# Memory attention and a bilinear FFN on one core: turning the means of k and v by DMA instead of on TensorE

## The chip, the cores and the metric

The kernel runs on one core of one Trainium2 chip. The metric is the device time of one execution in microseconds (us); it was run three times. A core has five engines that work side by side, each on its own list of instructions, in order: TensorE (PE, matmuls; its weight loads are shown apart as PEld), VectorE (DVE), ScalarE (ACT), GpSimd (POOL) and SyncE (SP, which here only issues DMAs). PE writes to PSUM, which has eight banks; DVE and ACT read results from there. DMAs are issued by SyncE, ScalarE or GpSimd and carried by 16 DMA engines.

## The reference, cut to what matters

There are 8 batches, 8 heads, 576 tokens, head size 64 and 32 memory slots. `phi` decides how the tokens are averaged into 32 slots; attention then runs over those slots, and its output goes through two up projections, whose product goes through the down projection.

```python
a = np.exp(phi - np.max(phi, axis=2, keepdims=True))
a = a / (np.sum(a, axis=2, keepdims=True) + 1e-09)
k_m = np.einsum('bhsm,bhsd->bhmd', a, k)        # means of k: 32 x 64 for each head
v_m = np.einsum('bhsm,bhsd->bhmd', a, v)        # means of v
scores = scale * np.matmul(q, k_m.transpose(0, 1, 3, 2))
attn = softmax(scores)                          # over the 32 slots
x = np.matmul(attn, v_m)                        # then (B, S, H*D)
out = ((x @ w_a) * (x @ w_b)) @ w_out           # d_model 512, d_ff 1536
```

## The kernel before: the parts that matter here

The kernel never forms `x`. It multiplies the means of v into the up weights ("fold"), so that the up projection of a batch is the attention matrix `A` times a folded weight `vab`. Both the scores (which need the means of k) and the fold (which needs the means of v) take them with the head dimension on the partitions, so the means have to be turned. For batches 2 to 7 this is a chain of three units:

```python
def kv_sums():                      # "kv": 72 small matmuls, exp(phi) x (k, v, ones), into two PSUM banks
    t["pkv"] = [banks.take([P, 3, D], F32, "pkv", hold=True) for _ in range(2)]
    for i in range(NI):
        for g in range(2):
            for j in range(4):
                r, hp = head(g, j)
                nc.tensor.matmul(t["pkv"][g][0][32 * j:32 * j + 32], ..., tile_position=(64 * r, 32 * j))

def take_kv():                      # "km": divide by the sums, PSUM -> SBUF, on VectorE; frees the two banks
    t["rep"] = mid.tile([P, 2, 3, P], F16, name="rep")
    for g in range(2):
        pkv, bank = t["pkv"][g]
        nc.vector.reciprocal(out=t["rphi"][:, g:g + 1], in_=pkv[:, 2, 0:1])
        ...                         # two tensor_scalar: 128 x 256 and 128 x 128
        banks.free(bank)

def kv_transpose():                 # "kvt": six 128 x 128 transposes on TensorE, one VectorE copy out of PSUM
    t["kvT"] = mid.tile([P, 6, P], F16, name="kvT")
    pT = banks.tile([P, 6, P], F16, name="pT")
    for g in range(2):
        for x in range(3):
            nc.tensor.transpose(out=pT[:, ...], in_=t["rep"][:, g, x], identity=ident)
    nc.vector.tensor_copy(out=t["kvT"], in_=pT)
```

The matmuls of `kv`, of the fold (`v0` to `v2`) and of the scores (`sc`) use small tiles of the PE array (64 x 32 or 32 x 32 instead of 128 x 128). The fold and the scores read `kvT`:

```python
def fold(lo, hi, zs):               # "v0", "v1", "v2": 16 matmuls into four held banks
    if len(zs) > 1 and b > 2:
        work.settle()               # first bring the down product that holds a second bank to its end
    ...
def take_fold(lo, hi, z):           # "x0a" ... "x2b": one copy on ScalarE, one on VectorE; frees two banks
    for g, engine_copy in enumerate((nc.scalar.copy, nc.vector.tensor_copy)):
        ...
def scores(gs):                     # "sc": 32 matmuls into four held banks; "e0", "e1" take two each on ScalarE
```

The main loop is the up projection, half a batch at a time in 12 steps. One step is two matmuls `pa`, two matmuls `pb`, a copy of `pa` on ScalarE (`a_sb`) and a product on VectorE (`ht`). After each step come some matmuls of the down projection (`py`, `pv`, `px`; `work.advance`), and then the side units that the plan has in that slot. The side units prepare the next batch; a name with `'` is of the batch after that one. `qt` turns q on VectorE, `exp` is the exponential of phi, `den` and `nr` make the softmax's denominators, and `L` issues the loads of a later batch.

```python
for step in steps:
    for _ in up(*step):
        work.advance()
        next(side, us[step[0]]["-"])()

second = "v2_+x2a_+exp0 x2b_ exp1 - kv+km qt0 kvt+qt1 - qt2+qt3 sc+e0 e1+v0+x0a+x0b den0 ... x2b - qt2'+nr1+kv'+km' - - kvt'+qt3'"
every = "- sc+e0 e1 den0 v0+x0a+x0b - - nr0+exp0' - - v1+x1a qt0' x1b+den1 exp1' - v2+x2a+x2b nr1+qt1' kv'+km' qt2' - qt3' - kvt'+L -"
last = "sc+e0 - e1 - v0+x0b - x0a den1 - - den0 v1+x1b x1a+nr0 - - - - nr1+v2+x2a - - - - - x2b"
```

`second` runs during batch 2, `every` during batches 3, 4 and 5, `last` during batch 6. So the means of batches 3 and 4 are made in `second`, those of batches 5, 6 and 7 in `every` (`kv'`, `km'`, `kvt'`). PSUM banks are handed out in program order, the one freed longest ago first.

Of the kernel before, what the change touches and what calls it, by code (L numbers as in the profile page):

```python
# [8 lines left out]
F32 = mybir.dt.float32  # L9
F16 = mybir.dt.float16  # L10
# [3 lines left out]
P = 128  # L14
# [4 lines left out]
def kernel(  # L19
# [11 lines left out]
    nc = tc.nc  # L31
# [14 lines left out]
    mid = ctx.enter_context(tc.tile_pool(name="mid", bufs=2))  # L46
    small = ctx.enter_context(tc.tile_pool(name="small", bufs=2))
# [105 lines left out]
    ident = consts.tile([P, P], F16, name="ident")  # L153
# [32 lines left out]
    def units(b):  # L186

        u = {}
        t = {}
# [28 lines left out]
                            tile_position=(64 * r, 32 * j),  # L218
                        )

        def take_kv():

            t["rep"] = mid.tile([P, 2, 3, P], F16, name="rep")
            t["rphi"] = small.tile([P, 2], F32, name="rphi")
            for g in range(2):
                pkv, bank = t["pkv"][g]
                nc.vector.reciprocal(out=t["rphi"][:, g:g + 1], in_=pkv[:, 2, 0:1])
                km = pkv[:, 0].rearrange("p (d e) -> p e d", e=2).unsqueeze(2).to_broadcast([P, 2, 4, 32])
                vm = pkv[:, 1].unsqueeze(1).to_broadcast([P, 2, D])
                for out, x in ((t["rep"][:, g, 0:2].rearrange("p e (z d) -> p e z d", z=4), km),  # L230
                               (t["rep"][:, g, 2].rearrange("p (z d) -> p z d", z=2), vm)):
                    nc.vector.tensor_scalar(out=out, in0=x, scalar1=t["rphi"][:, g:g + 1], scalar2=None, op0=ALU.mult)
                banks.free(bank)

        def kv_transpose():

            t["kvT"] = mid.tile([P, 6, P], F16, name="kvT")
            pT = banks.tile([P, 6, P], F16, name="pT")
            for g in range(2):
                for x in range(3):  # L240
                    nc.tensor.transpose(out=pT[:, (2 * g + x, 4 + g)[x == 2], :], in_=t["rep"][:, g, x], identity=ident)
            nc.vector.tensor_copy(out=t["kvT"], in_=pT)

        def sums(g, x):

            if g == 0 and x == 0:
                t["kvm"] = mid.tile([P, 2, 2, D], F16, name="kvm")
                t["rphi"] = small.tile([P, 2], F32, name="rphi")
                t["kvT"] = mid.tile([P, 6, P], F16, name="kvT")
            part = (slice(0, 3, 2), slice(1, 2))[x]  # L250
            pk = banks.tile([P, 2 - x, D], F32, name="pk")
# [3 lines that stand above are left out]
                    nc.tensor.matmul(  # L255
                        pk[32 * j:32 * j + 32],
                        t["exp"][64 * r:64 * r + 64, hp, i, :],
                        kvs[b][64 * r:64 * r + 64, part, hp, D * i:D * (i + 1)],
                        start=(i == 0),
                        stop=(i == NI - 1),  # L260
                        tile_position=(64 * r, 32 * j),
                    )
            if x == 0:
                nc.vector.reciprocal(out=t["rphi"][:, g:g + 1], in_=pk[:, 1, 0:1])
            nc.vector.tensor_scalar(out=t["kvm"][:, g, x], in0=pk[:, 0], scalar1=t["rphi"][:, g:g + 1], scalar2=None,
                                    op0=ALU.mult)
# [86 lines left out]
        def one(f, *a):  # L353
            return lambda: f(*a)

        for z in range(2):
            u[f"exp{z}"] = one(exp_phi, z)
            u[f"ks{z}"] = one(sums, z, 0)
            u[f"kt{z}"] = one(transpose, z, 0)
            u[f"vs{z}"] = one(sums, z, 1)  # L360
            u[f"vt{z}"] = one(transpose, z, 1)
            u[f"s{z}"] = one(scores, (z,))
            u[f"e{z}"] = one(exp_scores, z)
            u[f"den{z}"] = one(denominators, z)
            u[f"nr{z}"] = one(normalise, z)
            for hf in range(2):
                u[f"den{z}{hf}"] = one(denominators, z, (hf,))
                u[f"nr{z}{hf}"] = one(normalise, z, slice(hf, hf + 1))
            for n in range(NCH):
                u[f"v{n}{'ab'[z]}"] = one(fold, 512 * n, 512 * (n + 1), (z,))  # L370
                u[f"x{n}{'ab'[z]}"] = one(take_fold, 512 * n, 512 * (n + 1), z)
            for n in range(2):
                u[f"hv{n}{'ab'[z]}"] = one(fold, 256 * n, 256 * (n + 1), (z,))
                u[f"hx{n}{'ab'[z]}"] = one(take_fold, 256 * n, 256 * (n + 1), z)
# [4 lines left out]
        u["sc"] = one(scores, (0, 1))  # L379
        u["kv"] = one(kv_sums)  # L380
        u["km"] = one(take_kv)
        u["kvt"] = one(kv_transpose)
        u["-"] = lambda: None
        return u

# [230 lines left out]
    def ups(steps, side=()):  # L616

        side = iter(side)
# [4 lines that stand above are left out]
        for f in side:  # L623
            work.advance()
            f()
# [5 lines left out]
    def half_steps(b, hf, lo=0):  # L631

        return [(b, i, (hf,)) for i in range(lo, NFF)]

    us = {b: units(b) for b in range(B)}

    def named(b, names):
# [6 lines left out]
    def slots(b, names):  # L644

        def both(fs):
            return lambda: [f() for f in fs]
        def unit(n):
            if n == "fin":
                return lambda: work.pull(-work.done % NFF)  # L650
            if n == "L":
                return lambda: load(b + 2) if b + 2 < B else None
            if n[0] == "y":
                return lambda: some(int(n[1:]))
            if n[0] == "d" and n[1:].isdigit():
                return lambda: work.pull(int(n[1:]))
            return us[b + n.endswith("'") - n.endswith("_")][n.rstrip("'_")]

        return [both([unit(n) for n in x.split("+")]) for x in names.split()]
# [30 lines left out]
    ups(half_steps(1, 0, 4), slots(1, "- v2a+x2a+v2b+x2b+qt0' - - qt1'+exp0' exp1'+qt2' - kv'+km'+y9"))  # L690
    work.plan(S + HALF, 10)
    ups(half_steps(1, 1, 4), slots(2, "qt3 kvt - sc+e0+e1 - den0+den1+nr0 - v0+nr1+x0a x0b - v1+x1b x1a"))
    second = "v2_+x2a_+exp0 x2b_ exp1 - kv+km qt0 kvt+qt1 - qt2+qt3 sc+e0 e1+v0+x0a+x0b den0 nr0+v1+x1a - x1b+exp0' L exp1' v2+x2a den1+qt0'+qt1' x2b - qt2'+nr1+kv'+km' - - kvt'+qt3'"
    every = "- sc+e0 e1 den0 v0+x0a+x0b - - nr0+exp0' - - v1+x1a qt0' x1b+den1 exp1' - v2+x2a+x2b nr1+qt1' kv'+km' qt2' - qt3' - kvt'+L -"
    last = "sc+e0 - e1 - v0+x0b - x0a den1 - - den0 v1+x1b x1a+nr0 - - - - nr1+v2+x2a - - - - - x2b"
    for b in range(2, B):
        if b == 2:
            load(4)
# [35 lines left out]
```

The softmax here doesn't subtract the row's maximum and nothing guards it: scores larger than these inputs give would overflow.

## Time and profile before

| | before |
|---|---|
| time, median of three (lowest to highest) | 243.41 us (243.34 to 243.49) |
| span of the profiled execution | 241.9 us |
| DMA: moved, mean rate | 34.12 MB, 141 GB/s |
| HBM read / written | 42.47 MB / 9.44 MB |
| copy of the turned means out of PSUM, 128 x 768 (DVE) | 6 times, median 554 ns |
| products of the means, `rep` (DVE) | 24 times, median 413 ns |
| loads of phi, k, v, q of one batch (issued by GpSimd) | 576 KB each; median issue to landing 6.8, 9.5, 10.2, 13.5 us |
| store of an output row block (issued by SyncE) | 128 KB, median 3.1 us |

An engine's busy time says how much of the span it worked. The chain of work is the one that ended last, followed back from the last instruction; each piece of it names an engine, the tile written and the source line, and `x72` is the number of instructions in the piece. A piece whose length is more than its instructions need holds a wait or a switch. In this trace the line numbers are those of the kernel before: L212 is the sums of k and v, L241 the transposes on TensorE, L292 the scores, L338 the fold, L466 the down products, L594 the up matmuls.

### The profile page before, as it was taken

What the parts mean: (1) busy time and instruction counts of PE and PEld (TensorE: products, weight loads), DVE (VectorE), ACT (ScalarE), POOL (GpSimd) and SP (SyncE); (2) the same over time, 40 slices, a digit from 0 to 9 for tenths busy, and PEclk for the clock granted to TensorE, in tenths of its full rate; (3) what the DMA queues carried; (4) which work ended last, traced back from release to release, by engine and by line L of the source; (5) the groups of instructions that cost most, each with busy time, mean ns of one, the idle gap of its engine ahead of it and who ended that gap; (6) DMA issues with size and microseconds to landing.
All of it is one profiled execution on the core that took longest, in us unless ns stands there. A gap on an engine that the chain in (4) does not pass through costs nothing.

```text
span 241.9 us, 7803 instructions
## 1 busy us (share of the span) xinstructions
PE 230.9 (95%) x3110; PEld 169.8 (70%) x3110; DVE 167.2 (69%) x406; ACT 157.2 (65%) x410; POOL 159.4 (66%) x135
## 2 busy tenths in 40 slices
PE   7769999999999999999999999999999999999993
PEld 7535664456757867777788777877787878888882
DVE  4635784569858869976984659875987586756642
ACT  2265761669697599598857777587856877565330
POOL 7953244599879539973989759882949087936001
PEclk9999999999999999999999999999999999999999
DMA  6999999999947943992269542795220303032154
GB/s 235 234 197 207 206 256 207 256 208 283 219 130 178 217 91 93 235 194 49 46 174 212 140 89 56 170 207 137 49 46 12 78 13 78 8 84 63 42 129 116
DMA packets 25764, 34.12 MB, mean 141 GB/s; under 512 B 2016, under 2 KB 19808, under 8 KB 25728
## 3 DMA queue, kind: packets, MB, share of 16 engines
q0 software_dynamic: 19264, 23.14, 51.6%
q1 hardware_dynamic: 5952, 9.70, 15.8%
q10 hardware_dynamic: 512, 0.79, 1.0%
q8 instruction: 24, 0.39, 0.7%
q14 instruction: 12, 0.10, 0.1%
HBM read 42.47 MB, written 9.44 MB: 215 GB/s over the span
## 4 chain that ended last, share of the span: by engine, by line
PE 88%; ACT 4%; DMA 3%; DVE 2%; issue 2%; DVEq 0%; POOLq 0%
PE pa L594 20%; PE pb L594 19%; PE py L466 17%; PE pv L466 8%; PE pva L338 5%; PE po L391 5%; PE px L466 4%; DMA phi_sb<-in_phi_dram 3%; PE pkv L212 2%; PE pscore L292 2%; PE pD L315 1%; PE pk L255 1%; ACT E L305 1%; ACT L L316 1%; PE pw L151 1%
## 5 line engine op out<-in xcount | busy, mean ns | idle before, releaser
L605 DVE TENSOR_TENSOR ht<-a_sb,pb 128x288 f16<-128x288 f16 x168 | 73.3, 448 | 36.2 <-ACT a_sb L602 26.9
L594 PEld LDWEIGHTS <-vab 128*128 128x128 f16 x768 | 71.5, 98 | 27.3 <-issue 9.4
L602 ACT CAST a_sb<-pa 128x288 f16<-128x288 f32 x168 | 66.9, 409 | 26.2 <-PE pa L594 24.7
L594 PE MATMUL pa<-A,vab 128*128 128x288 f16 x384 | 75.9, 287 | 0.2
L594 PE MATMUL pb<-A,vab 128*128 128x288 f16 x384 | 74.9, 286 | 1.0 <-ACT vab L350 0.5
L448 POOL TENSOR_TENSOR h_sums<-ht 128x768 f16<-128x768 f16 x28 | 45.9, 1642 | 32.9 <-DVE ht L605 32.5
L466 PEld LDWEIGHTS <-h_sums 128*128 128x128 f16 x384 | 37.3, 98 | 7.0 <-issue 0.5
L350 DVE CAST vab<-pva 128x512 f16<-128x512 f32 (+1 forms) x52 | 32.6, 644 | 4.6 <-PE pva L338 4.2
L350 ACT CAST vab<-pva 128x512 f16<-128x512 f32 (+1 forms) x52 | 28.1, 571 | 9.4 <-PE pva L338 9.2
L466 PEld LDWEIGHTS <-ht 128*128 128x128 f16 x288 | 28.1, 98 | 5.7 <-issue 0.4
L466 PE MATMUL py<-w_sums,h_sums 128*128 128x256 f16 x192 | 30.4, 272 | 0.0
L448 POOL TENSOR_TENSOR h_sums<-ht,h_sums 128x768 f16<-128x768 f16 x14 | 23.0, 1643 | 0.9
L448 POOL TENSOR_TENSOR h_sums<-h_sums,ht 128x768 f16<-128x768 f16 x14 | 23.0, 1642 | 0.9
L326 POOL TENSOR_TENSOR A<-E,R 128x576 f16<-128x576 f16 x12 | 15.3, 1279 | 7.5 <-ACT R L324 7.4
L305 ACT ACTIVATE E<-pscore 128x288 f16<-128x288 f32 x32 | 11.4, 417 | 12.3 <-PE pscore L292 12.2
L466 PE MATMUL pv<-w_sums,h_sums 128*128 128x256 f16 x96 | 16.2, 273 | 0.0
L466 PE MATMUL py<-wo_sb,ht 128*128 128x256 f16 x96 | 16.0, 273 | 0.0
L473 ACT ACTIVATE u<-py 128x256 f32<-128x256 f32 x32 | 12.6, 393 | 5.0 <-PE py L466 4.8
L466 PE MATMUL py<-w_sums,ht 128*128 128x256 f16 x96 | 15.5, 272 | 0.1
L466 PE MATMUL px<-wo_sb,ht 128*128 128x256 f16 x96 | 15.4, 273 | 0.0
L316 ACT ACTIVATE L<-pD 128x288 f32<-128x288 f32 x32 | 11.6, 429 | 5.1 <-PE pD L315 4.8
L194 ACT ACTIVATE exp_sb<-phi_sb 128x576 f16<-128x576 f32 x16 | 11.0, 705 | 5.6 <-DMA phi_sb<-in_phi_dram 5.6
(65 smaller groups left out, 280.5 us busy)
## 6 DMA issues: line engine op xcount, KB each, us to landing
out_dram<-o_sb SPq DMA_DIRECT2D x68, 128.0 KB, 3.1
phi_sb<-in_phi_dram POOLq DMA_DIRECT2D x8, 576.0 KB, 6.8
kv_sb<-in_v_dram POOLq DMA_DIRECT2D x7, 576.0 KB, 10.2
kv_sb<-in_k_dram POOLq DMA_DIRECT2D x7, 576.0 KB, 9.5
q_sb<-in_q_dram POOLq DMA_DIRECT2D x6, 576.0 KB, 13.5
wo_sb<-in_moe_w_out_dram POOLq DMA_DIRECT2D x6, 256.0 KB, 13.6
q_sb<-in_q_dram POOLq DMA_DIRECT2D x4, 288.0 KB, 10.0
wa_sb<-in_moe_w_a_dram POOLq DMA_DIRECT2D x2, 512.0 KB, 13.8
```

Of the source, the lines that this page charges most:

```text
L305: nc.scalar.activation(out=Ev[:, g, :, z, :], in_=pss, func=AF.Exp, scale=1.0 / (8.0 * CS))
L316: nc.scalar.activation(out=t["L", g][:, sl], in_=pD, func=AF.Ln)
L326: engine.tensor_tensor(out=attn[b][:, g, sl], in0=t["E"][:, g, sl], in1=t["R", g][:, sl], op=ALU.mult)
L338: nc.tensor.matmul(t["pva", lo, z][g][0][32 * j:32 * j + 32, 0:hi - lo], t["kvT"][64 * r:64 * r + 64, 4 + g, M * j:M * j + M], w_sbs[z][64 ...
L350: engine_copy(out=vabs[b][z][:, g, lo:hi], in_=pva[:, 0:hi - lo])
L391: nc.tensor.matmul(po, ht[:, i, P * c:P * (c + 1)], wo_sb[:, i, :], start=(i == 0), stop=(i == NFF - 1))
L448: engine.tensor_tensor(out=out, in0=in0, in1=in1, op=op)
L466: nc.tensor.matmul(po, lhs[:, i], rhs[:, i], start=first and i == 0, stop=i == KH - 1, skip_group_check=not first)
L473: nc.scalar.mul(out=x, in_=po, mul=scale)
L594: nc.tensor.matmul(ps, vabs[b][x][:, g, P * i:P * (i + 1)], attn[b][:, g, HALF * hf:HALF * (hf + 1)], start=(g == 0), stop=(g == 1))
L602: nc.scalar.copy(out=a_sbs[b, i, hf], in_=ps)
L605: nc.vector.tensor_tensor(out=ht[:, i, t0:t0 + HALF], in0=a_sbs.pop((b, i, hf)), in1=ps, op=ALU.mult)
```

## The change

The turn of the means of batches 5, 6 and 7 leaves TensorE. A new unit `kvd` issues one DMA transpose on SyncE's queue, from `rep` in SBUF to `kvT` in SBUF; `rep` gets the six blocks in the order of `kvT`, so that one transfer of 128 x 768 does all. The unit `km` can now be done one bank at a time (`km0`, `km1`). In `every`, the sums `kv'` come directly behind the fold `v1`, seven slots earlier than before, so that the transfer has time and so that two groups of 64 x 32 matmuls stand in one run. The other side units are placed anew in all three plans: `d1` to `d5` pull that many matmuls of the down projection into a slot. Batches 2 to 4 keep the transposes on TensorE.

```diff
-        def take_kv():
-            t["rep"] = mid.tile([P, 2, 3, P], F16, name="rep")
-            for g in range(2):
+        def take_kv(gs=range(2)):
+            if gs[0] == 0:
+                t["rep"] = mid.tile([P, 6, P], F16, name="rep")
+                t["rphi"] = small.tile([P, 2], F32, name="rphi")
+            for g in gs:
 ... (same operations; rep is now indexed 2 * g, 2 * g + 1 and 4 + g)
-            for g in range(2):
-                for x in range(3):
-                    nc.tensor.transpose(out=pT[:, (2 * g + x, 4 + g)[x == 2], :], in_=t["rep"][:, g, x], identity=ident)
+            for x in range(6):
+                nc.tensor.transpose(out=pT[:, x, :], in_=t["rep"][:, x], identity=ident)
             nc.vector.tensor_copy(out=t["kvT"], in_=pT)
+
+        def kv_turn():
+            t["kvT"] = mid.tile([P, 6, P], F16, name="kvT")
+            nc.sync.dma_start_transpose(out=t["kvT"], in_=t["rep"].rearrange("p x d -> p (x d)"))
+            u[f"km{z}"] = one(take_kv, (z,))
+        u["kvd"] = one(kv_turn)
-    second = "v2_+x2a_+exp0 x2b_ exp1 - kv+km qt0 kvt+qt1 - qt2+qt3 sc+e0 e1+v0+x0a+x0b den0 nr0+v1+x1a - x1b+exp0' L exp1' v2+x2a den1+qt0'+qt1' x2b - qt2'+nr1+kv'+km' - - kvt'+qt3'"
-    every = "- sc+e0 e1 den0 v0+x0a+x0b - - nr0+exp0' - - v1+x1a qt0' x1b+den1 exp1' - v2+x2a+x2b nr1+qt1' kv'+km' qt2' - qt3' - kvt'+L -"
-    last = "sc+e0 - e1 - v0+x0b - x0a den1 - - den0 v1+x1b x1a+nr0 - - - - nr1+v2+x2a - - - - - x2b"
+    second = "v2_+d1+x2a_+exp0 x2b_ exp1 - kv+km+d2 qt0 d4+kvt+qt1 - qt2+qt3+sc+e0 - e1+v0+d2+x0a+x0b den0+d3 exp0' v1+nr0+x1a x1b+qt0' L+d5 den1 v2+x2a exp1'+qt1'+x2b - - qt2'+kv'+nr1+km' - - qt3'+kvt'+d5"
+    every = "- sc+e0 e1 den0 nr0+v0+x0a+x0b - - exp0' exp1' - v1+x1b+x1a+kv'+km0'+d3 - den1+km1' kvd'+qt0' - - nr1+qt1' v2+x2a+x2b - qt2' - qt3' - - L"
+    last = "sc+e0 d3 - e1 v0+x0b - - den1 - - den0+d1 x0a+v1+x1b x1a+nr0 - - - v2+x2a - nr1 - - - - x2b"
```

More of the change, by code (lines that the diff above doesn't have):

```diff
@@ L219, in kv_sums @@
                         )
-        def take_kv():
-            t["rep"] = mid.tile([P, 2, 3, P], F16, name="rep")
-            t["rphi"] = small.tile([P, 2], F32, name="rphi")
-            for g in range(2):
+        def take_kv(gs=range(2)):
[3 more added lines that the diff above has]
+            for g in gs:
                 pkv, bank = t["pkv"][g]
@@ L229, in take_kv @@
                 vm = pkv[:, 1].unsqueeze(1).to_broadcast([P, 2, D])
-                for out, x in ((t["rep"][:, g, 0:2].rearrange("p e (z d) -> p e z d", z=4), km),
-                               (t["rep"][:, g, 2].rearrange("p (z d) -> p z d", z=2), vm)):
+                for out, x in ((t["rep"][:, 2 * g:2 * g + 2].rearrange("p e (z d) -> p e z d", z=4), km),
+                               (t["rep"][:, 4 + g].rearrange("p (z d) -> p z d", z=2), vm)):
                     nc.vector.tensor_scalar(out=out, in0=x, scalar1=t["rphi"][:, g:g + 1], scalar2=None, op0=ALU.mult)
```

## The prediction, made before the changed kernel was run

> **What bounds the kernel now.** I read the page's busy times first, then the chain that ended last by engine, then a table of stages, and then the chain itself, piece by piece, in two stretches.
>
> ```profile
> PE 230.9 (95%) x3110; PEld 169.8 (70%) x3110; DVE 167.2 (69%) x406; ACT 157.2 (65%) x410; POOL 159.4 (66%) x135
> ...
> PE 88%; ACT 4%; DMA 3%; DVE 2%; issue 2%; DVEq 0%; POOLq 0%
> ```
>
> TensorE is busy 95% of the span and carries 88% of the chain; the other engines stand at 65 to 70%. The stages (batch 2; its end; batches 3, 4, 5; 6 and 7; the tail) say where that holds:
>
> ```profile
> 72.50:87.00 14.50, 14.42 (x237) 10.60 (x235) 12.24 (x31) 10.28 (x28) 9.66 (x9) 1.00 0.99 201
> ...
> 101.00:127.00 26.00, 26.00 (x351) 19.95 (x350) 20.73 (x51) 19.41 (x51) 19.48 (x15) 1.00 0.59 123
> 127.00:155.00 28.00, 28.00 (x371) 21.86 (x369) 19.49 (x48) 19.73 (x52) 23.78 (x18) 1.00 0.61 122
> 155.00:181.00 26.00, 26.00 (x351) 19.82 (x349) 20.30 (x49) 19.61 (x53) 15.73 (x11) 1.00 0.59 125
> ```
>
> From 101 to 181 us PE is busy for every microsecond at full clock. No wait is left there to take away: what gets shorter there must be work of PE, or time that PE loses between two kinds of work. The chain shows both (start, length, engine, tile, line):
>
> ```profile
> 117.00 0.56 PE pva L338 x16
> 117.56 0.35 PE pa L594 x2
> 117.91 0.24 PE pb L594 x2
> 118.16 0.33 PE py L466 x3
> ...
> 119.30 0.87 PE pkv L212 x72
> 120.17 0.35 PE pa L594 x2
> 120.52 0.24 PE pb L594 x2
> ...
> 124.36 0.34 PE pT L241 x6
> 124.70 0.25 PE pa L594 x2
> ```
>
> A pair `pa` takes 0.24 us, but 0.35 right behind the small tiles of the fold or of the sums: leaving the small tiles costs 0.11. Behind the transposes it takes 0.25: 128 x 128 transposes cost no switch. In the same pattern for batches 6 and 7 the transposes stand at 154.22 and 179.48, again 0.34 long.
>
> The second stretch is batch 2, the only place after 75 us where the chain leaves PE before the tail:
>
> ```profile
> 84.63 0.40 PE pscore L292 x31
> ...
> 85.05 0.12 ACT E L305
> ...
> 85.76 0.30 ACT a_sb L602
> ...
> 86.09 0.47 DVE ht L605
> ...
> 86.59 0.41 PE pa L594 x2
> ```
>
> After the scores PE had one step (0.35 + 0.24) and a fold (0.56) to do, which ends at 85.03 + 1.15 = 86.18; it goes on at 86.59. So some 0.4 us are lost to the row exponentials, the copy and the product that must free PSUM banks.
>
> **What the Trainium skill says.** TensorEngine Tiling (Array Packing), section Tiling Modes: changing the tiling mode drains TensorE. The trace agrees: 0.11 us on leaving; the fold and the sums are both 64 x 32, so one behind the other should not drain. TensorE: Matmul & The Clock Gate, Part 4: PE-mode transpose: the output lands in PSUM and has to be copied, and one 128 x 128 transpose took about 275 ns in a kernel. Here six back to back take 0.34 us together, 57 ns each, and the measurement decides; the copy is there (554 ns on DVE). DMA: Bandwidth & Descriptors, section Latency and other measured facts: DMA transposes reached 261 GB/s with strided blocks, 350 to 400 when contiguous. No run here shows one yet. The same page, section Queues, rings and completion order: an engine serves the queues in turn, packet by packet, so that a transfer shares with the loads.
>
> **The change part by part.**
>
> *Transposes off PE.* Three groups of six transposes, 0.34 us each, all on the bounding engine: 3 x 0.34 = 1.02 us less. Three DVE copies of 0.55 go too (1.7 us of DVE), off the path and worth nothing by themselves.
>
> *Sums behind the fold.* In the new order of PE's instructions the 72 matmuls stand directly behind the 16 of `v1`, three times. Entering and leaving is paid once for both. Leaving is 0.11. Entering I take from the run itself: a group of eight 64 x 32 matmuls works side by side, a `pa` of 288 columns takes 0.12 us, so 0.42 ns a column; 72 x 192 / 8 columns are 0.72 us, and the run takes 0.87: 0.15 over. For the fold, 16 x 512 / 8 columns are 0.43 and the run takes 0.56: 0.13 over. So one pair of switches is 0.24 to 0.26 us, and 3 x 0.25 = 0.75 us go.
>
> *Batch 2.* Scores now stand one slot before the fold with an empty slot between, two products follow the fold and three the denominators. This should take most of the 0.4 us wait: 0.3 us less. The rest of `second` has no wait to remove.
>
> *What is moved and costs nothing if it fits.* The `d` units do not add matmuls, they take them from later slots. 3110 matmuls become 3092, the 18 transposes. The last 108 matmuls, behind the last up step, are in the same order as before, with their wait of about 1.3 us on DVE at 226 us; the tail stays. So does the start: up to 72 us nothing that runs is changed.
>
> *The DMA transpose.* 128 x 768 x 2 bytes are 197 KB. At the skill's 261 GB/s that is 0.75 us, to which I add the 3.1 us from issue to landing of a 128 KB store: an estimate of 3 to 5 us. The room it has: in batch 3 the fold `v1` stands at 112.34, so the sums run from 112.9 to 113.7. In the kernel before the products of `km` end 2.7 us after the sums begin (119.30 to 122.0); now the second half comes two slots later, about 4 us after: 117. The scores come at 128.46 less what was saved, say 127.5: 10 us of room. Batch 6: sums at 142.8, products done at 147, scores at 157.12 less 1.5: 8.5 us. Batch 7: 168, 172, and scores at 181.78 less 2: nearly 8 us. An estimate of 3 to 5 us fits in all three. The stores behind it on SyncE's queue come later by as much; four output buffers, two used per pair of blocks, leave them that time.
>
> *Inputs.* The sums come seven slots earlier, so k and v must have landed earlier. The load for batch 7 is issued from 152.1 to 155.2, and GpSimd's place for it hardly moves. The DMA share by stretches of 3 us is 1.19 at 162 to 165 and 0.40 at 165 to 168, so the last of the four (q) lands near 166 and v before; the sums want it at 168. For batch 5 the share is 0.02 from 111 on, wanted at 112.9; for batch 6 it falls to 0.47 from 135 on, wanted at 142.8. It fits, by 2 to 6 us.
>
> Sum: 1.02 + 0.75 + 0.3 = 2.1 us less, 241.3.
>
> **The rivals.**
>
> *The transfer is slow or delayed.* If turning 197 KB takes 12 us rather than 4, the scores wait about 2, 3.5 and 4 us, some 10 us together, because PE is in order and has no slack: 251. Against it speaks the care with which `kv'` was moved forward: nobody gives eight slots to a transfer of 2 us, but that also says that it is not short. For it speaks that no row of this profile shows a DMA transpose; and for batch 5 a transfer beyond 5 us would meet the load issued at 122.3 on all engines.
>
> *A pile-up behind `v1`.* Slot 10 now holds two copies on DVE (1.28), two on ACT (1.12), and the first half of the products (0.9 on DVE), the second half follows two slots later. A step needs 0.45 us of DVE in about 0.85. Counted from the end of the fold, DVE is done with the copies at 1.28, with the first half at 2.2, with two `ht` at 3.1, with the second half at 4.0. PE meanwhile does the sums (0.83), three products, two steps, two more products and the denominators, until 2.7. Its banks come free just ahead of it: the third step's `pb` needs the bank of the first `ht`, free at 2.65, and gets to it at 2.95. That fits by 0.3 us. If it does not, 0.3 us are lost three times, with like delays at slot 4, where `nr0` joins the copies on ACT: 242.5 in all.
>
> *Banks in `last`.* `x0a` now comes seven slots after its fold, so two more banks are held, and only four are left for the steps. The same count leaves 0.15 to 0.3 us a step. A loss here would be below 1 us.
>
> *The bound does not move but other waits grow with it.* DVE loses 1.7 us of work and ACT none, both below 75%, so no other engine becomes the bound.
>
> **Range and chances.** 241.3 if all fits; I add 0.3 for small waits that a new plan nearly always brings: 241.6 us, 0.7% less. The low end is all of the sum and all of the batch-2 wait, 240.8. The high end has the pile-up and one late transfer, 244.0. Faster by over 2% means under 238.5, more than there is to remove: 0.02. Slower by over 2% (above 248.3) needs the slow transfer: 0.05. Within 2%: 0.93.
>
> **What would show it.** In the chain after: no `pT` pieces after 105 us; `pkv` directly behind `pva`, the two together near 1.3 us, with one 0.35-like exit behind; PE at 100% in the stages of batches 3 to 5, each about 0.6 us shorter. The row of the DMA transpose should land in 3 to 5 us. I am wrong if `pscore` waits for `kvT`, if `pkv` waits for a load or for `exp`, or if `pa` or `pb` in the two steps behind `v1` wait for `rep`, `vab` or `ht`.

## The result and the profile after

The changed kernel takes 241.28 us (median of four, 241.15 to 241.93) against 243.38 us before: a ratio of 0.9919, 95% interval 0.9900 to 0.9937. The prediction was 241.6 us, in a range of 240.8 to 244.0.

Three lines of the profile of the changed kernel: busy times, the hardware DMA queue (packets, MB, share of 16 engines) and, from the table of DMA issues, the new transfer (count, median us from issue to landing).

```profile
PE 230.6 (96%) x3092; PEld 170.3 (71%) x3092; DVE 165.4 (69%) x403; ACT 158.7 (66%) x410; POOL 159.5 (67%) x135
...
q1 hardware_dynamic: 8352, 10.29, 18.4%
...
kvT<-rep SPq DMA_TRANSPOSE x3, 3.3
```

The 18 matmuls that are gone are the transposes. The queue carries 2,400 packets more than before (5,952), 800 for each transfer of 197 KB: they are small.

Two executions can stand up to a microsecond apart at a place that has the same work behind it (the sums of batch 3 begin at 77.66 us before, at 77.41 after, and between 77.2 and 78.2 in the runs below). For effects of 0.3 us the whole time is too coarse. So I compare two stretches, each between the starts of two pieces of the chain. Stretch A runs from the sums of batch 3 to the scores of batch 4, stretch B from there to the scores of batch 7. First the kernel before (both), then the one after (both): start and end, length and PE busy, the other engines' busy times, then PE's clock, DMA share and GB/s.

```profile
77.66:102.25 24.59, 24.51 (x415) 18.46 (x418) 21.13 (x55) 18.20 (x47) 17.93 (x14) 1.00 0.79 160
102.25:181.78 79.53, 79.53 (x1078) 61.26 (x1083) 59.63 (x144) 58.40 (x153) 58.47 (x43) 1.00 0.59 121
```

```profile
77.41:102.04 24.63, 24.55 (x418) 18.61 (x423) 21.19 (x55) 18.25 (x47) 18.28 (x15) 1.00 0.82 163
102.04:179.68 77.64, 77.64 (x1056) 60.49 (x1062) 57.71 (x140) 59.30 (x153) 58.16 (x42) 1.00 0.66 130
```

B is 1.89 us shorter, and PE is busy all the time in both. The two kernels do not have the same work in a stretch: by the order of PE's instructions, A has 74 down products before and 77 after, B 291 and 288 (the `d` units). Three products are 0.33 us in the chain. For the same work A is 0.29 us shorter and B 1.56 us: 1.85 us together. From the scores of batch 7 to the wait in the tail, both take 44.37 us. The rest of the difference of the medians, 2.10 us, is of the size by which the starts differ.

The chain of the changed kernel, at the place where fold and sums now meet:

```profile
111.79 0.56 PE pva L343 x16
112.35 0.76 PE pkv L212 x70
113.11 0.43 PE py L473 x3
```

The sums take 0.76 us here instead of 0.87, and only one exit is paid, by the products behind them (0.43 instead of 0.33). The list of SyncE in the same stage, and then the landings of the three transfers (least, median, most):

```profile
116.23 2.08 SPq L247 DMA_TRANSPOSE kvT<-rep  x1
```

```profile
DMA to landing us min/median/max: 2.7/3.3/3.7
```

The scores of batch 5 come at 127.37 us, so the transfer of batch 5 had 11.1 us and used 3.3; the 3.7 are of batch 6.

### The profile page after: what moved, and what is told of

The parts are those of the page before. It is cut to its first block, busy times and chain, and to the rows that moved or that the text cites. A ratio compares the mean times of both kernels' runs of the same rounds, so it can differ in the third digit from the quotient of the medians.

```text
span 239.6 us, 7764 instructions
## 1 busy us (share of the span) xinstructions
PE 230.6 (96%) x3092; PEld 170.3 (71%) x3092; DVE 165.4 (69%) x403; ACT 158.7 (66%) x410; POOL 159.5 (67%) x135
## 3 DMA queue, kind: packets, MB, share of 16 engines
q0 software_dynamic: 19264, 23.14, 52.2%
## 4 chain that ended last, share of the span: by engine, by line
PE 77%; DMA 16%; DVE 2%; issue 1%; POOL 1%; ACT 1%; DVEq 0%; POOLq 0%
PE py L473 18%; PE pa L601 18%; PE pb L601 17%; PE pv L473 9%; DMA wb_sb<-in_moe_w_b_dram 6%; DMA q_sb<-in_q_dram 5%; PE pva L343 5%; DMA kv_sb<-in_v_dram 4%; PE px L473 4%; PE po L398 2%; PE pkv L212 2%; PE pscore L297 1%; PE pD L320 1%; DVE ht L612 1%; ACT a_sb L609 1%
## 5 line engine op out<-in xcount | busy, mean ns | idle before, releaser
L601 PEld LDWEIGHTS <-vab 128*128 128x128 f16 x768 | 72.4, 98 | 24.9 <-issue 7.8
L473 PE MATMUL py<-w_sums,h_sums 128*128 128x256 f16 x192 | 31.3, 273 | 0.0
L473 PE MATMUL py<-wo_sb,ht 128*128 128x256 f16 x96 | 16.7, 273 | 0.0
L473 PE MATMUL px<-wo_sb,ht 128*128 128x256 f16 x96 | 15.9, 273 | 0.0
L321 ACT ACTIVATE L<-pD 128x288 f32<-128x288 f32 x32 | 11.5, 418 | 6.0 <-PE pD L320 5.8
L203 DVE STREAM_TRANSPOSE qT<-q_sb 128x288 f32<-128x288 f32 x32 | 14.6, 464 | 0.3 <-DMA q_sb<-in_q_dram 0.3
## 6 DMA issues: line engine op xcount, KB each, us to landing
kv_sb<-in_v_dram POOLq DMA_DIRECT2D x7, 576.0 KB, 10.3
```

The lines of the kernel that those rows point to most:

```text
L203: nc.vector.transpose(out=t["qT"][:, hp, :].bitcast(F32), in_=qs[b][:, hp, :].bitcast(F32))
L321: nc.scalar.activation(out=t["L", g][:, sl], in_=pD, func=AF.Ln)
L473: nc.tensor.matmul(po, lhs[:, i], rhs[:, i], start=first and i == 0, stop=i == KH - 1, skip_group_check=not first)
L601: nc.tensor.matmul(ps, vabs[b][x][:, g, P * i:P * (i + 1)], attn[b][:, g, HALF * hf:HALF * (hf + 1)], start=(g == 0), stop=(g == 1))
```

## The experiments

All runs are variants of the changed kernel; only the plans of the side units are edited. "Stretch A" and "B" are those above, and a comparison is always for the same number of down products, or says so. A few executions, of the kernel before too, ran part of their time at a lower clock and took 257 to 261 us; medians, ranges and ratios leave them out, and since the recorded execution of `e2_split` is one of them, its positions stand some 16 us later, with stretch B at full clock.

### The yardstick

No edit.

> The changed kernel once more, as the yardstick for the runs beside it: 241.3 us, 2.1 us below the kernel before.

Measured: 241.50 us (241.23 to 242.00), ratio 0.9922, interval 0.9908 to 0.9936; stretch A 24.62 us, B 77.64 us. The whole time moves by 0.8 us from one execution to the next, the stretches by 0.01 us between two recorded executions.

### What the transposes cost

```diff
-den1+km1' kvd'+qt0' - - nr1+qt1'
+den1+km1' qt0' - kvt' nr1+qt1'
```

> Only the way of turning goes back for batches 5 to 7: six TensorE transposes and a VectorE copy, three slots after the sums' second half, in place of the DMA. Theory (the transposes cost what they take on TensorE): 3 x 0.34 = 1.0 us above the changed kernel, 242.3 us, with pieces of 0.34 us and no wait. Rival (the DMA transpose gives part of this back, by contention or by the order of stores): less than 0.5 us above. Other rival (what counts was the VectorE copy in a crowded stage): clearly more than 1.0 us, 1.5 or above.

Measured: 242.42 us (242.25 to 243.10), 0.92 us above the yardstick; ratio to before 0.9959, interval 0.9944 to 0.9974. Stretch B of this run, and one of its three transposes in the chain:

```profile
102.57:181.22 78.65, 78.65 (x1075) 61.50 (x1081) 58.74 (x143) 59.31 (x153) 58.17 (x42) 1.00 0.59 121
```

```profile
117.98 0.34 PE pT L241 x6
118.31 0.24 PE pa L601 x2
```

B is 78.65 against 77.64 us with the same work: 1.01 us for three groups, 0.337 each, and the pieces read 0.34. The DMA transpose itself gives nothing of it back, and the copy on VectorE cost nothing. Both rivals fall.

### What the run of fold and sums saves

```diff
-v1+x1b+x1a+kv'+km0'+d3
+v1+x1b+x1a+d1+kv'+km0'+d2
```

> One down product of the three behind the sums is moved between the fold and the sums, three times; nothing else changes. Theory (leaving and entering the small tiles costs TensorE a drain each way): 3 x 0.22 = 0.66 us above the changed kernel, 241.9 us, with the sums back at 0.87 us and 0.11 more for the product behind the fold. Rival (the run as a whole is no shorter for being in one piece, the gain came from elsewhere): within 0.15 us of the changed kernel.

Measured: 241.77 us (241.74 to 241.92), 0.27 us above the yardstick, ratio 0.9930, interval 0.9917 to 0.9944, which overlaps that of the yardstick: the whole time does not decide. The trace does. Its stretch B, and the place in the chain:

```profile
118.21:196.47 78.26, 78.26 (x1056) 60.27 (x1062) 58.02 (x140) 59.31 (x153) 58.18 (x42) 1.00 0.63 129
```

```profile
127.96 0.56 PE pva L343 x16
128.52 0.21 PE py L473
128.73 0.87 PE pkv L212 x72
129.60 0.33 PE py L473 x2
```

One product between the two, with no other change, makes B 0.62 us longer: 0.21 a place. It is in the pieces: the product takes 0.21 instead of 0.11 (leaving the fold's tiles), and the sums take 0.87 instead of 0.76 (entering them again). So the cost sits in the switch, and the rival that the run as such saves nothing falls.

### What the new plan of batch 2 saves

```diff
-    second = (the plan of the changed kernel)
+    second = (the plan of the kernel before)
```

> Only the plan of batch 2 goes back to what it was. Theory (the new plan there removes most of a wait of 0.4 us at the scores of batch 3): 0.3 us above the changed kernel, 241.6 us, with the piece of the row exponentials back in the chain near 85 us. Rival (the wait only changes its place, since the chain of the changed kernel still leaves TensorE at 84.9 us for 0.95 us): no difference, within 0.1 us.

Measured: 241.60 us (241.47 to 242.32), 0.10 us above the yardstick, ratio 0.9928, interval 0.9914 to 0.9942: not to be told apart by the whole time. Stretch A is 24.60 us, as in the kernel before (24.59), with 74 products; the changed kernel needs 24.62 or 24.63 with 77. For the same work that is 0.3 us. Here are the scores of batch 3 in the chain of the changed kernel:

```profile
83.85 0.40 PE pscore L297 x31
84.25 0.35 PE pa L601 x2
84.60 0.26 PE pb L601 x2
...
84.87 0.41 ACT a_sb L609
...
85.30 0.47 DVE ht L612
...
85.81 0.41 PE pva L343 x8
```

The row exponentials are out of this chain, but it still goes over a copy and a product before the second half of the fold. The two steps and the fold would end at 85.88 us (84.25 + 0.35 + 3 x 0.24 + 0.56) and end at 86.22: 0.34 us are lost. In the kernel before, the loss here was 0.47 (0.41 of waiting, and the next `pa` took 0.41 instead of 0.35), so only 0.13 us are won at this place. Most of the rest is one `pb` two steps behind the fold, which takes 0.24 us in the changed kernel; with the old plan it reads

```profile
88.09 0.36 PE pb L601 x2
```

and the transposes of batch 3 take 0.38 us instead of 0.34. Together these make 0.29 us. So the size that the theory named is there, in the trace only, but less than half of it comes from the wait that it named; whether the other pieces follow from that wait is not shown.

### How much room the transfer needs

```diff
-den1+km1' kvd'+qt0' - - ... qt3' - - L
+den1 qt0' - - ... qt3' km1' kvd' L
```

> The second half of the products (km1') and the DMA transpose come ten slots later, at slots 22 and 23 of each batch; everything else stays. In the changed kernel the transpose is issued at 116.2, 145.7 and 170.3 us, takes about 3.3 us to land, and the scores come at 127.4, 155.7 and 179.7: 7.4, 6.7 and 6.2 us are left. Theory (the transfer is hidden only because it was given that room): a slot is about 0.93 us, so it comes 9.3 us later and the scores wait 1.9, 2.6 and 3.1 us, together 7.6: 249 us. Rival (the loads that are issued at the end of batches 3 and 4 share the DMA engines with it): longer landings in those two, 5 us or more, and none such for the last, 251 us or above. Other rival (a transfer of 3 us finds its place anyway): under 243 us.

Measured: 267.45 us (265.60 to 268.49), ratio 1.098, interval 1.094 to 1.102. That is far above the 249 us of the theory; only the first rival, with no upper end, allows it. The chain of this run at the scores of batch 5, and at those of batch 7 (a DMA's piece runs from its issue to its landing):

```profile
124.91 10.27 DMA kvT<-rep
...
135.22 0.71 PE pscore L297 x28
135.94 0.59 PE pa L601 x2
...
201.44 2.73 DMA kvT<-rep
...
204.22 0.48 PE pscore L297 x32
```

The timeline of PE gives the idle time ahead of the same scores:

```profile
135.22 0.71 PE L297 MATMUL pscore<-qT,kvT 32*32 32x288 f16 x32 [7.97 <-DMA kvT<-rep]
```

```profile
204.22 0.48 PE L297 MATMUL pscore<-qT,kvT 32*32 32x288 f16 x32 [2.12 <-DMA kvT<-rep]
```

For batch 7 the transfer lands in 2.7 us and the scores wait 2.1 us; 3.1 were expected. For batches 5 and 6 the same transfer takes 10.3 and 10.5 us, and PE stands still for 7.97 and 9.21 us. What differs is the load: during batches 3 and 4 GpSimd issues the load of a later batch, during batch 5 nothing is left to load. In batch 3, where the transfer goes out at 124.91, the four issues are:

```profile
122.70 0.81 POOL L78 DMA_DIRECT2D phi_sb<-in_phi_dram  x1
...
124.98 0.75 POOL L90 DMA_DIRECT2D q_sb<-in_q_dram  x1
```

So the first rival was right, longer landings beside a load and none for the last, and they are twice its least, 5 us. The waits make 7.97 + 9.21 + 2.12 = 19.3 of the 26.4 us by which the two spans differ (266.0 and 239.6). The rest is of the size of what PE's clock takes: it is below full speed behind each of the three waits (last section), with means of 0.85 over 135 to 152 us, 0.78 over 175 to 189 and 0.72 over 204 to 210, which makes an estimate of 2.6 + 3.1 + 1.7 = 7.4 us.

### Whether the products had to be split in two

```diff
-kv'+km0'+d3 - den1+km1' kvd'
+kv'+km'+d3 - den1 kvd'
```

> Both halves of the products directly behind the sums (one unit again), the rest as in the changed kernel. Theory of the pile-up (the halves were split because VectorE is then too late with the products ht that free PSUM banks; by the count of banks the third step has 0.3 us to spare, and the second half costs 0.9): PE waits 0.4 to 0.6 us three times, 1.2 to 1.8 us above the changed kernel, 242.6 to 243.2 us, with VectorE in the chain behind the sums. Rival (the bank freed two slots earlier makes up for it, or VectorE's lag is absorbed): within 0.2 us of the changed kernel.

Measured: 243.42 us (243.14 to 244.15), as slow as the kernel before and slower than the theory had it: ratio 1.0004, interval 0.9990 to 1.0017. Its stretch B, and the place in the chain:

```profile
101.82:181.52 79.70, 78.17 (x1057) 60.35 (x1063) 58.57 (x140) 59.57 (x153) 58.08 (x42) 1.00 0.62 127
```

```profile
114.53 0.12 PE pD L320
...
114.88 0.35 DVE rep L233
...
115.28 0.42 PE pa L601 x2
```

B is 2.06 us longer, 0.69 a place. PE has the matmuls of the denominators behind it and waits until VectorE has written the second half of `rep`, not for an `ht` as the theory had it; the same piece stands at 145.00 and 170.36. The pile-up is real, and the split `km0`, `km1` is what keeps the gain of the other parts. In the changed kernel VectorE's list at this place reads:

```profile
112.45 1.29 DVE L355 CAST vab<-pva 128x512 f16<-128x512 f32 x2
113.65 0.16 DVE L228 RECIPROCAL rphi<-pkv 128x1 f32<-128x1 f32 x1
113.85 0.74 DVE L233 TENSOR_SCALAR rep<-pkv,rphi 128x256 f16<-128x256 f32 x2
114.51 0.81 DVE L612 TENSOR_TENSOR ht<-a_sb,pb 128x288 f16<-128x288 f16 x2
115.23 0.16 DVE L228 RECIPROCAL rphi<-pkv 128x1 f32<-128x1 f32 x1
115.43 0.74 DVE L233 TENSOR_SCALAR rep<-pkv,rphi 128x256 f16<-128x256 f32 x2
```

Two `ht` get between the halves, and with them two banks.

### Batch 4 too: the sums behind a fold

```diff
-L+d5 den1 v2+x2a exp1'+qt1'+x2b - - qt2'+kv'+nr1+km' - - qt3'+kvt'+d5
+L+exp1' den1 v2+x2b+x2a+kv'+km0'+d3 - qt1'+km1' - qt2'+nr1 kvt' - qt3'+d5
```

> Batch 4 as well: its sums come directly behind the fold v2 of batch 3, its transposes stay on TensorE. Theory: one more pair of switches saved, 0.22 us below the changed kernel, 241.2 us; in the trace the stretch from the sums of batch 3 to the scores of batch 4 is 0.22 us shorter for the same work. Rival (v2, x2b, x2a and the first half of the products in one slot pile up on VectorE and ScalarE): a wait of the same size or larger eats it.

Measured: 241.62 us (241.44 to 242.56), ratio 0.9936, interval 0.9917 to 0.9954, no better than the changed kernel. Stretch A is 24.88 us against 24.63, both with 77 products; 24.41 was expected. The chain shows a wait before the sums:

```profile
92.49 0.26 PE pb L601 x2
...
92.79 0.46 ACT a_sb L609
...
93.27 0.47 DVE ht L612
...
93.77 0.92 PE pkv L212 x68
```

Behind this `pb`, which ends at 92.75, PE has three products (0.33 us) and the fold (0.56) to do and could begin the sums at 93.64. Most of them begin at 93.77 and end at 94.70, where 0.76 us without a wait would have ended at 94.40: 0.30 us are lost, more than the switch saves. Another 0.14 is a `pb` at 98.10 that takes 0.38 instead of 0.24. The chain comes from the `ht` of the last step and not from the VectorE copies, as the rival had it; it fits a PSUM bank that the sums take and that this `ht` still has to free. In batches 3 to 5 twelve products stand before the fold (six `py` and six `pv` in the order of the instructions), and here three.

### Batch 4 too: by DMA

```diff
-L+d5 den1 v2+x2a exp1'+qt1'+x2b - - qt2'+kv'+nr1+km' - - qt3'+kvt'+d5
+L+exp1' den1 v2+x2b+x2a+kv'+km0'+d3 km1' kvd' qt1' qt2'+nr1 - - qt3'+d5
```

> Batch 4 as well: sums behind v2 and the turn by DMA, six slots (about 5.5 us) before its scores. Theory: 0.22 + 0.34 = 0.56 us below the changed kernel, 240.9 us, as issue to landing takes 3.3 us. Rival (the landing is later behind stores or beside a load, 5 us or more): the scores of batch 4 wait 0.5 us or more, and the gain is gone.

Measured: 250.42 us (249.69 to 250.78), ratio 1.028, interval 1.026 to 1.030. The transfer again, in the chain:

```profile
97.09 11.45 DMA kvT<-rep
```

It was issued at 97.09; GpSimd had issued the load of batch 5 from 94.01 to 97.04. The landing took 11.5 us, and the scores of batch 4 waited 6.90 us for it.

### Products ahead of the fold

```diff
-v2+x2b+x2a+kv'+km0'+d3 - qt1'+km1'
+d4+v2+x2b+x2a+kv'+km0' - qt1'+km1'
```

> The sums of batch 4 behind the fold v2 again, but with four down products ahead of the fold, so that the product ht of the last step has freed its bank when the sums want it. In the run before, the sums waited 0.46 us there and the stretch from the sums of batch 3 to the scores of batch 4 was 24.88 us against 24.63 of the changed kernel. Theory (that wait was the bank): with 0.44 us more ahead it is nearly gone, and the stretch is 24.4 to 24.5 us; the whole about 0.2 us below the changed kernel, 241.3 us. Rival (the wait was for something else, and follows): 24.8 us or more again.

Measured: 241.77 us (241.66 to 242.69), ratio 0.9935, interval 0.9917 to 0.9953, stretch A 25.09 us, longer than without the four products ahead. The 0.46 us in the expectation leave out the three products behind the `pb`; the loss there was 0.30. That wait is gone, as the theory said: the sums follow the fold at 94.89 us and take 0.76. But the third step behind them now waits for `rep`, with no product of the down projection between the sums and the first step any more:

```profile
97.18 0.42 PE L601 MATMUL pa<-A,vab 128*128 128x288 f16 x2 [0.34 <-DVE rep L233]
```

The theory named the wait rightly and was wrong on what follows, so that the stretch came out in the rival's range.

### The load out of the way

```diff
-x1b+qt0' L+exp1' den1 d4+v2+x2b+x2a+kv'+km0' - qt1'+km1' - qt2'+nr1 kvt' - qt3'+d5
+x1b+qt0' exp1' den1 d4+v2+x2b+x2a+kv'+km0' km1' kvd' nr1 L+qt1' qt2' - qt3'+d5
```

> As the last one, with the turn of batch 4 by DMA, and the load that was in its way moved behind nr1, so that GpSimd issues it near 99 us, when the transfer of 97 us is about to land. Theory (the transfer took 11.5 us only because the load of batch 5 was in flight; alone it lands in 2.7 to 3.3 us): landing under 4 us, no wait at the scores of batch 4, and 0.22 + 0.34 us below the changed kernel, 240.9 us. Rival one (the stores or the place in the queue made it slow): a landing of 8 us or more and 248 us or above again. Rival two (the load now comes too late for the sums of batch 5, wanted near 112 us; v lands some 12 us after the first issue): the sums of batch 5 wait up to 1 us, and the gain is lost.

Measured: 241.39 us (241.19 to 242.39), ratio 0.9924, interval 0.9903 to 0.9946: 9 us below the run with the load ahead. The transfer was issued at 97.51 us and the first load at 99.02. The landing of the transfer of batch 4:

```profile
DMA to landing us min/median/max: 2.9/2.9/2.9
```

2.9 us instead of 11.5, from the same source to the same place in nearly the same stage, and no wait at the scores. Stores and queue stayed as they were, so rival one falls; the sums of batch 5 do not wait either (the chain goes from the fold to the sums at 112.38 without a gap), so rival two falls. The expected gain over the changed kernel is not there: the third step's wait for `rep` (0.35 us of VectorE in the chain) is the same as in the run before, and A takes 24.75 us. Against that run A is 0.34 us shorter, which is just the group of transposes.

### A version that has all of it

```diff
-d4+v2+x2b+x2a+kv'+km0' km1' kvd' nr1 L+qt1' qt2'
+d3+v2+x2b+x2a+kv'+km0'+d3 - km1' kvd'+nr1 L+qt1' qt2'
```

> Batch 4 by DMA with its load behind nr1, and down products on both sides of fold and sums (three and three), the second half of the products one slot later. In the run before, the sums no longer waited but the third step behind them did, 0.43 us, for the first half of the products, since no down product stood between; the stretch to the scores of batch 4 was 24.75 us. Theory (three products there, 0.33 us, cover most of it): 24.4 us, 241.2 us. Rival (VectorE, with two copies, the products and three ht behind each other, is the limit of this slot in batch 3, however PE is filled): 24.7 us or more.

> The changed kernel beside it, as yardstick: 241.3 to 241.5 us, and 24.63 us from the sums of batch 3 to the scores of batch 4.

Measured side by side: 241.16 us (241.06 to 241.66) and, for the changed kernel, 241.31 us (241.19 to 241.76); ratios to before 0.9907 (0.9892 to 0.9921) and 0.9912 (0.9898 to 0.9926). Stretch A of the two:

```profile
77.56:101.93 24.37, 24.21 (x411) 18.39 (x417) 20.55 (x54) 17.98 (x47) 16.36 (x13) 1.00 0.63 121
```

```profile
77.47:102.10 24.63, 24.55 (x417) 18.61 (x424) 21.18 (x55) 18.25 (x47) 18.28 (x15) 1.00 0.81 164
```

The stretch is 0.26 us shorter for the same 77 products, as the theory had it. By the whole time it is the lowest median of all, but the intervals overlap, so "faster than the changed kernel" is shown for the stretch and not for the whole. Of the 0.56 us that batch 4 could give, half is still lost to VectorE behind the sums (the chain goes over its copies and `rep` from 94.2 to 96.4 us).

## Why the prediction was right

*Transposes off PE, 1.02 us.* Right: 1.01 us in stretch B when they alone come back.

*Sums behind the fold, 0.75 us.* The mechanism was right, the size too large: 0.62 us. Leaving costs the 0.11 us that were read from the chain. The mis-sized term is the entering, worked out as 0.13 to 0.15 us from the columns; one product in between showed 0.11 (0.87 against 0.76). The rest of that surplus does not go with the switch.

*Batch 2, 0.3 us.* Right in size, 0.29 to 0.31 us for the same work, and only seen because the products in the stretch were counted: the bare stretch is 0.04 us longer. The reason was right in part only. "Most of the 0.4 us wait" did not go: 0.13 of 0.47 us did, and the other 0.16 came from pieces that the prediction did not name. That the sum came to 0.3 is partly luck.

*New small waits, 0.3 us.* Smaller. B shortened by 1.56 us, where the transposes and the switches, measured apart, make 1.01 + 0.62 = 1.63: some 0.07 us went to new waits. The chain has one: three `py` at 131.56 us take 0.49 us, 0.16 too long, where the kernel before lost 0.06 ahead of the same fold.

*The sum.* The parts seen in the trace make 1.85 us, not the 2.1 that were added up. The medians differ by 2.10, 1.90 and 2.15 us in the three times that the pair was run, and in the recorded executions 0.25 us of the difference stand before stretch A. That the first median fell on the bare sum of 241.3 is therefore luck; 241.6 was as good a forecast. The low end of the range, 240.8, does not follow from its own words: 243.41 less 1.02, 0.75 and 0.4 is 241.2.

*Tail and start.* Right: 44.37 us from the scores of batch 7 to the wait in the tail, twice.

*The DMA transpose, 3 to 5 us.* Landed in 2.7 to 3.7 us, so the estimate was good for a transfer that is alone. The room was underrated: from its issue to the scores it had 11.1, 10.1 and 9.3 us. But the first rival was nearer than its chance said, and the prediction had its cause in half a sentence: a transfer that meets the load on all engines. The load of batch 6 was issued 3.4 us after the transfer of batch 5 had landed (119.5 and 122.9 us). With all three transfers ten slots later, two of them met a load and the kernel lost 26 us.

*The pile-up behind `v1`.* The count of VectorE's work, 1.28, 2.2, 3.1 and 4.0 us behind the fold, was right: the list above, counted from 112.35, gives 1.4, 2.2, 3.0 and 3.8. It fitted, by little: with both halves in one slot the kernel loses 2 us, all that the change had won.

*Banks in `last`, loads for the earlier sums.* No wait shows in the chain for either.

## What to carry to other kernels

When one engine is busy all the time, a gain is the sum of the pieces taken off it. Count the work of a stretch before comparing it, and compare stretches of two traces rather than whole times when the effect is below the spread of the runs. Matmuls of one tile size belong in one run: each switch in and out cost 0.2 us here. A DMA transpose of what used to go through TensorE was free here while no load was in flight beside it: place it so that it lands before the next load is issued, not merely some microseconds before its use. Work that keeps VectorE from freeing banks goes in halves.

## What was not expected of the hardware

*A transfer of small packets beside a load.* The same 197 KB landed in 2.7 to 4.6 us without a load beside it and in 10.3, 10.5 and 11.5 us with one. An estimate for the size of it: 800 packets are 50 for each of 16 engines, and 7.6 us of delay are 0.15 us for each; a packet of the loads takes 0.10 us on its engine (the software queue of the kernel before: 51.6% of 16 engines' 241.9 us over 19,264 packets). The Trainium skill, DMA: Bandwidth & Descriptors, section Queues, rings and completion order, has each engine take turns between the queues packet by packet. If what the profile counts as a packet is one of those, waiting for one packet of the loads before each of its own would explain two thirds of the delay. This is only argued: no run changed the packets' size.

*The clock after a wait.* Three stretches of 1 us in the run with the late transfer: inside the first wait, some time after it, and just after the third wait, which was short (PE's busy time is the second figure, its clock the third from the end):

```profile
130.00:131.00 1.00, 0.00 (x0) 0.00 (x0) 0.00 (x0) 0.00 (x0) 1.00 (x2) 0.50 1.20 197
...
140.00:141.00 1.00, 1.00 (x10) 0.78 (x9) 0.00 (x0) 0.55 (x2) 0.00 (x0) 0.93 0.18 43
...
205.00:206.00 1.00, 1.00 (x7) 0.71 (x5) 0.25 (x1) 0.71 (x3) 0.92 (x2) 0.50 0.00 0
```

PE's last matmuls end at 127.25 (135.22 less 7.97); the clock is halved from about 129.9 and comes back at about 140, some 5 us after PE went on at 135.2. The scores take 0.71 instead of 0.40 us, a pair `pa` 0.59 instead of 0.35. The third wait was only 2.12 us long, and the clock was halved all the same, from 205.0 to about 208.4, when PE was already at work again. Counted from the moment that PE stopped, the halving came 2.7, 4.8 and 2.9 us later in the three waits. The Trainium skill, TensorE: Matmul & The Clock Gate, section Part 1: The HAM clock gate, has such a halving after at least one idle window of about 3.4 us. The trace agrees on the half clock and not on that length: here a shorter wait was enough. By the estimate above, 19.3 us of waiting cost some 7 us more in this way.
